# Attention with a routed layer: one load queue with three loads under way, casts of q and k on GpSimd, stores on ScalarE's queue, whole-block transposes

## The chip, the core and the metric

The kernel runs on one core of a Trainium2 chip. The metric is the device time of one execution in microseconds. A core has five engines with an instruction queue each: TensorE (PE in the profile), VectorE (DVE), ScalarE (ACT), GpSimd (POOL) and SyncE (SP). Each queue is worked off in order. DMAs are issued from a queue (here SP, ACT or POOL) and carried out by 16 DMA engines that all queues share.

## The reference

There are 4 batches, 8 heads, 768 positions and 64 values per head. A position sees the first 4 positions (the sinks) and the last 128. After attention the heads are put side by side to x (768 x 512 per batch), and the 128 positions of each batch with the highest score x . w_gate go through a small network.

```python
scores = scale * np.matmul(q, k.transpose(0, 1, 3, 2))
keep = is_sink | in_window          # pos < 4, or 0 <= rel < 128
a = softmax(np.where(keep, scores, -1e9))
x = np.matmul(a, v)                 # heads side by side: (B, 768, 512)
for b in range(B):
    top_idx = np.argpartition(-s[b], 128)[:128]      # s = x . w_gate
    ye = np.maximum(x[b, top_idx] @ w1, 0.0) @ w2    # 512 -> 1024 -> 512
    out[b, top_idx] = x[b, top_idx] + sigmoid(s[b, top_idx])[:, None] * ye
```

## The kernel before

A batch is cut into six blocks of 128 positions, and its heads into four pairs; two pairs make a group g. A `unit(b, j, gs)` handles block j of batch b for the groups gs. Batch 0 runs its six blocks for group 0 and then for group 1; the other batches run both groups at once. The order on every engine is the order in which the functions are called, since all engines are scheduled by hand.

In a unit, `close()` ends the block before it (the products with the sinks on TensorE, then reciprocal, x and the gate's junk reduction on VectorE: L385, L388, L399). `scores` multiplies k and q of the next block on TensorE (L290, L307) and takes the exponentials on ScalarE (L313). `pv_halves` and `pv` multiply the exponentials with v (L365, L378). `transposes` brings q and k of one pair of the next batch into shape: TensorE transposes 24 halves into PSUM (L254), VectorE copies KT (L258) and ScalarE QT (L260), and GpSimd copies the sinks' columns of KT (L262). `spread` sends the gate scores along a row (L412, and L413 on ScalarE). In batches 1 to 3 the steps of choosing and of the network for the batch before are put between: `moe_steps` gathers the 128 rows from the output in DRAM with an indirect DMA of GpSimd (L462), and `mlp_steps` adds its result to them with another (L494).

Data come in so. The q and k of batch 0's first two pairs are loaded as fp32 on SP (`load`, L93), and cast by ScalarE and VectorE (`casts`, L139, L140). All other q and k, 28 loads, are cast to bf16 on the way by DMAs that GpSimd issues (L125). v is loaded by SP, 30 loads, into two buffers with a pitch of 128 fp32 values per head. The 16 blocks of w1 and w2 are loaded by SP and cast by GpSimd a unit later (`cast_w`, L240). The function `loads` holds a plan that names for every unit which loads it issues, and ties each to the last exponential, or the last product with v, that was issued ahead of it. The stores of x stand on SP as well (`finish_block`, L395, and L397 for a second copy of batch 3).

```python
def load(out, in_, flight=3, gate=None):
    ins = nc.sync.dma_start(out=out, in_=in_)
    if gate is not None:
        wait_for(ins, gate)
    elif len(line) >= flight:
        wait_for(ins, line[-flight])
    line.append(ins)
```

So a load without a gate waits for the load three (or four) places before it. The framework gives every DMA issued from SP or ACT one of eight completion semaphores in turn, and makes a DMA wait until the last one that held its semaphore is done.

Of the kernel before, what the change touches and what calls it, by code (L numbers as in the profile page):

```python
# [17 lines left out]
B = 4  # L18
H = 8
# [12 lines left out]
def kernel(  # L32
# [16 lines left out]
    wp = ctx.enter_context(tc.tile_pool(name="wp", bufs=1))  # L49
    qkp = ctx.enter_context(tc.tile_pool(name="qkp", bufs=2))  # L50
    qbp = ctx.enter_context(tc.tile_pool(name="qbp", bufs=6))
    vp = ctx.enter_context(tc.tile_pool(name="vp", bufs=1))
# [10 lines left out]


    vbuf = [vp.tile([128, NB, H, 2 * D], FP32, name=f"vbuf{i}", tag=f"vbuf{i}") for i in range(2)]
    vsr = [vp.tile([128, D], FP32, name=f"vsr{i}", tag=f"vsr{i}") for i in range(2)]
# [24 lines left out]

    def load(out, in_, flight=3, gate=None):
        ins = nc.sync.dma_start(out=out, in_=in_)  # L93
        if gate is not None:
            wait_for(ins, gate)
        elif len(line) >= flight:
            wait_for(ins, line[-flight])
        line.append(ins)
# [13 lines left out]

    def load_qk(st, hp, t, gate=None):
        nm, src = (("k", k), ("q", q))[t]
        ob = qbp.tile([128, 2, NB, D], BF16, name=nm + "b", tag=nm + "b")
        st.kq[hp, t] = ob
        in_ = src[st.b, 2 * hp:2 * hp + 2, :, :].rearrange("h (p c) d -> p h (c d)", c=NB)
        flat = "p h c d -> p h (c d)"  # L120
        if st.b == 0 and hp < 2:
            f = st.kf[hp, t] = qkp.tile([128, 2, NB, D], FP32, name=nm + "f", tag=nm + "f")
            load(out=f[:, :, :, :].rearrange(flat), in_=in_, flight=4)
        else:
            ins = nc.gpsimd.dma_start(out=ob[:, :, :, :].rearrange(flat), in_=in_)  # L125
            if gate is not None:
                wait_for(ins, gate)

    def load_v(st, c, hs, flight=3, gate=None):
        load(out=st.v[:, c, hs, 0:D], in_=v[st.b, hs, c * 128:(c + 1) * 128, :].rearrange("h p d -> p h d"),  # L130
             flight=flight, gate=gate)

# [4 lines left out]

    def casts(st, hp):
        nc.scalar.copy(out=st.kq[hp, 0][:, :, :, :], in_=st.kf[hp, 0][:, :, :, :])  # L139
        nc.vector.tensor_copy(out=st.kq[hp, 1][:, :, :, :], in_=st.kf[hp, 1][:, :, :, :])  # L140

# [8 lines left out]
    for hp in (0, 1):  # L150
        for t in range(2):
            load_qk(st0, hp, t)

# [41 lines left out]
    for c in (1, 2):  # L195
        load_v(st0, c, slice(0, 4))


# [33 lines left out]

    def load_w(i, gate):
        src = moe_w1[128 * (i // 2):, 512 * (i % 2):] if i < 8 else moe_w2[128 * (i - 8):, :]
        wf[i] = qkp.tile([128, 512], FP32, name="wf", tag="kf" if i % 2 else "qf")
        load(out=wf[i][:, :], in_=src[0:128, 0:512], gate=gate)

    def cast_w(i):
        dst = w1_sb[:, i // 2, 512 * (i % 2):512 * (i % 2) + 512] if i < 8 else w2_sb[:, i - 8, :]
        nc.gpsimd.affine_select(out=dst, in_=wf[i][:, :], compare_op=ALU.is_ge, fill=0.0,  # L240
                                base=0, pattern=[[0, 512]], channel_multiplier=0)

# [3 lines left out]
    def transposes(st, hp):  # L246
# [3 lines left out]
        for t, (src, dst) in enumerate(((st.kq[hp, 0], st.KT), (st.kq[hp, 1], st.QT))):  # L250
            trp = ps.tile([128, 8, 128], BF16, name="trp", tag="ps")
            for c in range(NB):
                for h in range(2):
                    nc.tensor.transpose(out=trp[es[h], c, :], in_=src[:, h, c, :], identity=ident_b[:])  # L254
            o = dst[:, hp, :].rearrange("d (p c) -> d p c", c=NB)
            i = trp[:, 0:NB, :].rearrange("d c p -> d p c")
            if t == 0:
                nc.vector.tensor_copy(out=o, in_=i)  # L258
            else:
                nc.scalar.copy(out=o, in_=i)  # L260
# [99 lines left out]
    def pv_halves(st, j, gs):  # L360
        for g in gs:
            for hh in range(4):
                for m in range(2):
                    f = first(st, j, g, m)
                    ins = nc.tensor.matmul(out=st.xg[j, g][es[m], hh, :],  # L365
                                           lhsT=prob(st, j - m, g, hh, es[m], 3 * m),
                                           rhs=st.v[es[m], j - m, 4 * g + hh, 0:VS], **f)
                    fence(st, j, gs, ins, 8 * gs.index(g) + 2 * hh + m, 8 * len(gs))
# [3 lines left out]
    def pv(st, j, g):  # L372
        terms = {0: [(0, 0), (0, 1)], 1: [(0, 2), (0, 3), (1, 0), (1, 1)]}.get(j, [(j - 1, 2), (j, 1)])
        for hh in range(4):
            for i, (kc, s) in enumerate(terms):
                m = i % 2
                f = first(st, j, g, m)
                late[0] = nc.tensor.matmul(  # L378
                    out=st.xg[j, g][es[m], hh, :], lhsT=prob(st, kc, g, hh, slice(0, 128), s),
                    rhs=st.v[:, kc, 4 * g + hh, 0:VS], **f)  # L380

    def normalize(st, j, g):
# [8 lines left out]
        if g == 1:  # L391
            finish_block(st, j)

    def finish_block(st, j):
        nc.sync.dma_start(out=out[st.b, j * 128:(j + 1) * 128, :], in_=st.x[j][:, :])  # L395
        if st.b == B - 1:
            nc.sync.dma_start(out=x_last[j * 128:(j + 1) * 128, :], in_=st.x[j][:, :])  # L397
        junk = mp.tile([128, DM], BF16, name="junk", tag="junk")
# [202 lines left out]


    qk_loads = {0: ([2], []), 1: ([3], [4]), 2: ([5], [6]), 3: ([7], [])}
    qk_loads_2 = {4: ([0], []), 5: ([1], [])}
    qk_loads_0 = {(i // 6, i % 6): ([i - 2], []) for i in range(2, 10)}

    w_loads = {(1, 3): 1, (1, 4): 1, (1, 5): 1, (2, 0): 1, (2, 2): 1, (2, 3): 1, (2, 4): 3, (2, 5): 3, (3, 0): 4}
    w_next = iter(range(16))
    w_casts = []

    def loads(b, j, gs, end):
        gate = late[0] if end else exps[-1]
        plans = [(b + 1, qk_loads.get(j) if b else qk_loads_0.get((gs[0], j)))]
        if 1 in gs:
            plans.append((b + 2, qk_loads_2.get(j)))
        for s, plan in plans:
            for i in plan[end] if plan and s < B else ():
                load_qk(states[s], i // 2, i % 2, gate)
        if end:
            for i in w_casts:  # L620
                cast_w(i)
            w_casts.clear()
            for _ in range(w_loads.get((b, j), 0)):
                i = next(w_next)
                load_w(i, gate)
                w_casts.append(i)
        nxt = states.get(b + 1)
        if end:
            return
        if b == 0:  # L630

            if gs == (0,) and j < 3:
                load_v(st0, j + 3, slice(0, 4), gate=gate)
            c = j - 2 if gs == (0,) else j + 4
            if 0 <= c < NB:
                load_v(st0, c, slice(4, 8), gate=gate)
        if nxt and 1 in gs:
            load_v(nxt, j, slice(0, H), gate=gate)
            if j == 0:
                load_sinks(nxt)  # L640

# [13 lines left out]
    def unit(b, j, gs):  # L655
        st = states[b]
        last = 1 in gs
        end = (b, j) == (B - 1, NB - 1)
        ahead = states.get(b + 1) if last else None
        close()  # L660
        if j == 0:
            for g in gs:
                scores(st, 1, g)
                pv(st, 0, g)
                normalize(st, 0, g)
            loads(b, j, gs, 0)
            pack_sinks(st, gs)
            sink_scores(st, gs)
        elif end:
# [7 lines left out]
            for g in gs:  # L677
                normalize(st, j, g)
            cast_x(st, j)
        else:  # L680
# [3 lines left out]
            elif ahead:  # L684
                scores(ahead, 0, 0)
            loads(b, j, gs, 0)
            if j >= 2:
# [24 lines left out]
        if b == B - 1 and j and not end:  # L712
            cast_x(st, j - 1)
        if last:
            loads(b, j, gs, 1)
        if ahead and j == 5:
# [6 lines left out]
    keep_warm(10)  # L723
    for hp in range(2):
        casts(st0, hp)
        transposes(st0, hp)
        for t in range(2):
            load_qk(st0, 2 + hp, t)
        keep_warm(3)
    scores(st0, 0, 0)  # L730
    wg_ps = ps.tile([128, DM], FP32, name="wg_ps", tag="ps")
    nc.tensor.matmul(out=wg_ps[:, :], lhsT=one[:, :], rhs=wg[:, :], start=True, stop=True)
    nc.vector.tensor_copy(out=wgb[:, :], in_=wg_ps[:, :])
    constants()
    for g in range(2):
        for j in range(NB):
            unit(0, j, (g,))
        if g == 0:
            scores(st0, 0, 1)
    for b in range(1, B):  # L740
        select[b - 1] = moe_steps(states[b - 1])
        mlp[b - 1] = mlp_steps(states[b - 1])
        for j in range(NB):
            unit(b, j, (0, 1))
# [36 lines left out]
```

## Time and profile before

| what | value |
|---|---|
| median of 3 runs (lowest to highest) | 148.12 us (146.75 to 152.5) |
| profiled execution: time, span | 147.8 us, 146.1 us |
| TensorE busy in matmuls | 126.4 us, 87% of the span |
| VectorE, ScalarE, GpSimd busy | 90.3, 78.8, 52.6 us |
| granted TensorE clock, mean | 0.971 |
| DMA queues: hardware, software | 19.96 MB at 47.4%, 7.21 MB at 34.7% of 16 engines' span |
| instruction transfers of 16 KB | 23 |
| matmuls and weight loads | 2,923 each |
| chain that ended last | PE 64%, issue 11%, ACT 9%, DMA 6% |

A row of a time line gives the start in us, the length in us, the engine, the line of the kernel, the operation, the tiles it writes and reads, and in brackets how long the engine was idle before and what ended that. "issue" there means that the profile shows nothing the engine waited for. A row of the list of groups gives the number of instructions, their busy time, the mean of one in ns, and the idle time before them. In the rows of windows come the length, the busy time and the number of instructions of PE, its weight loads, DVE, ACT and POOL, then the granted clock, the busy share of the DMA engines and GB/s. The rows of 40 slices give tenths, 3.65 us a slice.

### The profile page before, as it was taken

Reading aid. Unit: us, or ns where it says so; the run is one execution under the profiler, and the core shown is the slowest. Engines: PE = TensorE matmul, PEld = TensorE weight load, DVE = VectorE, ACT = ScalarE, POOL = GpSimd, SP = SyncE. Lnnn points to the kernel's source line nnn. Section 1 sums busy time; section 2 is a strip of 40 time slices with the busy share of each in tenths; the row PEclk is TensorE's granted clock in tenths of the full one; section 3 lists DMA queues with packets and bytes.
Section 4 is the critical chain, followed back from the end, with each engine's and each line's share of the span. In section 5 each row is a group of like instructions: output and inputs, shape, how many; then the busy total and the mean of one; then the engine's idle time right before and its main releaser. Section 6 shows DMA issues by size and latency. Waiting matters only on the chain.

```text
span 146.1 us, 6782 instructions
## 1 busy us (share of the span) xinstructions
PE 126.4 (87%) x2923; PEld 99.1 (68%) x2923; DVE 90.3 (62%) x294; ACT 78.8 (54%) x168; POOL 52.6 (36%) x111
## 2 busy tenths in 40 slices
PE   6859997996979999888999967799999999999900
PEld 2335886685867897777779846597896886586600
DVE  5635444565977987767699836376994624794120
ACT  3448552963658666653875823348763872542300
POOL 5467143142330525232251380405525240424320
PEclk9999999999999999999999999779999999999985
DMA  4969499399999899999759999966796456391701
GB/s 143 295 106 210 102 149 187 69 191 238 280 266 230 189 196 273 200 288 272 179 75 268 263 223 227 304 227 193 216 252 254 115 101 194 79 244 48 125 19 72
DMA packets 41600, 27.61 MB, mean 189 GB/s; under 512 B 26593, under 2 KB 35169, under 8 KB 41570
## 3 DMA queue, kind: packets, MB, share of 16 engines
q1 hardware_dynamic: 32930, 19.96, 47.4%
q0 software_dynamic: 8640, 7.21, 34.7%
q8 instruction: 23, 0.38, 1.0%
q14 instruction: 7, 0.06, 0.1%
HBM read 24.15 MB, written 8.91 MB: 226 GB/s over the span
## 4 chain that ended last, share of the span: by engine, by line
PE 64%; issue 11%; ACT 9%; DMA 6%; DVE 3%; POOLq 1%; SPq 1%; POOL 1%; ACTq 0%
PE xg L378 17%; PE xg L365 11%; PE trp L254 8%; ACT pt L313 7%; PE sc L290 7%; PE xg L350 6%; DMA qf<-in_q_dram 4%; PE sc L307 3%; PE bc L412 3%; PE hps L482 3%; PE ye L488 2%; DMA out_dram<-gye,idx 2%; DVE cm L418 1%; ACT psk L324 1%; SPq L93 1%
## 5 line engine op out<-in xcount | busy, mean ns | idle before, releaser
L313 ACT ACTIVATE pt<-sc 128x448 f32<-128x448 f32 (+2 forms) x96 | 44.4, 551 | 10.3 <-PE sc L307 9.9
L378 PE MATMUL xg<-vbuf,pt 128*64 128x65 f32 x896 | 34.4, 226 | 0.2 <-ACT pt L313 0.2
L378 PEld LDWEIGHTS xg<-vbuf,pt 128*64 128x64 f32 x896 | 29.4, 137 | 4.4 <-issue 1.6
L260 ACT COPY QT<-trp 128x768 bf16<-128x768 bf16 x16 | 12.8, 798 | 27.4 <-PE trp L254 27.4
L365 PE MATMUL xg<-vbuf,pt 64*64 64x65 f32 x512 | 22.1, 226 | 2.4 <-issue 2.0
L258 DVE COPY KT<-trp 128x768 bf16<-128x768 bf16 x16 | 15.3, 956 | 12.5 <-PE trp L254 12.5
L365 PEld LDWEIGHTS xg<-vbuf,pt 64*64 64x64 f32 x512 | 20.0, 140 | 3.2 <-issue 2.2
L290 PE MATMUL sc<-QT,KT 64*64 64x192 bf16 (+3 forms) x384 | 20.8, 255 | 0.8 <-issue 0.4
L388 DVE TENSOR_TENSOR x<-xg,rz 128x256 f32<-128x256 f32 x48 | 20.4, 424 | 1.7
L385 DVE RECIPROCAL rz<-xg 128x4 f32<-128x4 f32 x48 | 8.5, 176 | 19.3 <-PE xg L350 17.5
L307 PE MATMUL sc<-msk,ident_b 64*64 64x256 bf16 (+1 forms) x256 | 17.7, 258 | 0.2 <-issue 0.2
L399 DVE CUSTOM_DVE_ANT_0 junk<-x,wgb 128x512 bf16<-128x512 f32 x24 | 16.9, 706 | 0.8
L290 PEld LDWEIGHTS <-KT 64*64 64x64 bf16 x384 | 11.7, 107 | 8.0 <-issue 4.0
L125 POOL DMA_DIRECT2D kb<-in_k_dram x14 | 10.3, 734 | 16.1 <-ACT pt L313 16.1
L418 DVE SCALAR_TENSOR_TENSOR cm<-sbc,scol,tie 128x128 bf16<-128x128 f32 (+5 forms) x23 | 15.3, 664 | 0.1
L262 POOL TENSOR_SCALAR_AFFINE_SELECT ksk<-KT 64x4 bf16<-64x4 bf16 x32 | 6.0, 188 | 25.5 <-DVE KT L258 19.0
L240 POOL TENSOR_SCALAR_AFFINE_SELECT w_sb<-wf 128x512 bf16<-128x512 f32 x16 | 10.5, 662 | 12.9 <-DMA wf<-in_moe_w_dram 12.5
L254 PE MATMUL trp<-ident_b,kb 128*64 128x128 bf16 x192 | 9.1, 221 | 6.6 <-issue 5.3
L125 POOL DMA_DIRECT2D qb<-in_q_dram x14 | 10.1, 718 | 11.2 <-ACT pt L313 11.2
L350 PE MATMUL xg<-vsk,psk 64*64 64x260 f32 x128 | 13.9, 416 | 0.0
L254 PEld LDWEIGHTS <-kb 128*64 128x64 bf16 x192 | 6.4, 110 | 8.3 <-issue 5.9
L307 PEld LDWEIGHTS <-ident_b 64*64 64x64 bf16 x256 | 10.0, 109 | 0.5 <-issue 0.5
(113 smaller groups left out, 148.8 us busy)
## 6 DMA issues: line engine op xcount, KB each, us to landing
out_dram<-x SPq DMA_DIRECT2D x24, 256.0 KB, 4.2
vbuf<-in_v_dram SPq DMA_DIRECT2D x18, 256.0 KB, 4.5
wf<-in_moe_w_dram SPq DMA_DIRECT2D x16, 256.0 KB, 6.4
kb<-in_k_dram POOLq DMA_DIRECT2D x14, 192.0 KB, 5.8
qb<-in_q_dram POOLq DMA_DIRECT2D x14, 192.0 KB, 5.9
vbuf<-in_v_dram SPq DMA_DIRECT2D x12, 128.0 KB, 4.4
x_last<-x SPq DMA_DIRECT2D x6, 256.0 KB, 3.3
kf<-in_k_dram SPq DMA_DIRECT2D x2, 384.0 KB, 4.5
```

Of the source, the lines that this page charges most:

```text
L125: ins = nc.gpsimd.dma_start(out=ob[:, :, :, :].rearrange(flat), in_=in_)
L254: nc.tensor.transpose(out=trp[es[h], c, :], in_=src[:, h, c, :], identity=ident_b[:])
L258: nc.vector.tensor_copy(out=o, in_=i)
L290: nc.tensor.matmul(out=sc[e][es[kh], hh * w + q0:hh * w + q1], lhsT=st.KT[es[e], hp, k0 + 64 * kh:k0 + 64 * kh + 64], rhs=st.QT[es[e], hp, ...
L307: nc.tensor.matmul(out=sc[e][es[kh], o:o + 2 * w].rearrange("p (h s n) -> p h s n", h=2, n=64)[:, :, sq, :], lhsT=ident_b[es[e], es[e]], r ...
L313: exps.append(nc.scalar.activation(out=pt[:, e, 0:n], in_=sc[e][:, 0:n], func=ACT.Exp, scale=0.125))
L350: ins = nc.tensor.matmul(out=st.xg[j, g][es[m], :, :], lhsT=st.psk[es[g], q0:q0 + 64], rhs=st.vsk[es[g], :, :], **f)
L365: ins = nc.tensor.matmul(out=st.xg[j, g][es[m], hh, :], lhsT=prob(st, j - m, g, hh, es[m], 3 * m), rhs=st.v[es[m], j - m, 4 * g + hh, 0:VS ...
L378: late[0] = nc.tensor.matmul(out=st.xg[j, g][es[m], hh, :], lhsT=prob(st, kc, g, hh, slice(0, 128), s), rhs=st.v[:, kc, 4 * g + hh, 0:VS], ...
L388: nc.vector.tensor_tensor(out=st.x[j][:, 256 * g:256 * g + 256].rearrange("p (h d) -> p h d", h=4), in0=xg[:, :, 0:D], in1=rz[:, :, :].to_ ...
L399: nc.vector.tensor_tensor_reduce(out=junk[:, :], in0=st.x[j][:, :], in1=wgb[:, :], scale=1.0, scalar=0.0, op0=ALU.mult, op1=ALU.add, accum ...
L418: nc.vector.scalar_tensor_tensor(out=cm[:, :], in0=st.sbc[:, 0:n], scalar=st.scol[:, j:j + 1], in1=tie[:, S - n:S], op0=ALU.subtract, op1= ...
```

## The change

The loads of q and k are all plain fp32 loads on SP now. The whole of batch b + 1 is put on SP's queue at the start of batch b (`load_batch`): eight loads of q and k, then six of v, with the 16 blocks of the weights between v of batch 3. A load waits only for the load three places before it (four in two places of batch 0), and for its buffer. The casts of q and k, but those of the first two pairs, go to GpSimd (`cast`), two instructions a tensor, one unit ahead of the transposes. q and k are kept with the two heads of a pair side by side, so that TensorE transposes a whole block of 128 x 128 at once, 12 for a pair. v lies with a pitch of 65 values. The stores of batches 0 to 2 are issued from ScalarE's queue (`stores`), right after the exponentials of a unit; those of batch 3 stay on SP. Half of the casts of the weights go to ScalarE, and all 16 are made at three places. At the start, three warming matmuls are gone and the gate weights' matmul stands ahead of the first scores.

```diff
-    qkp = ...(name="qkp", bufs=2)   qbp = ...(name="qbp", bufs=6)
+    qkp = ...(name="qkp", bufs=6)   qbp = ...(name="qbp", bufs=3)
-    vbuf = [vp.tile([128, NB, H, 2 * D], FP32, ...) for i in range(2)]
+    vbuf = [vp.tile([128, NB, H, VS], FP32, ...) for i in range(2)]
...
-    def load_qk(st, hp, t, gate=None):
...
-        if st.b == 0 and hp < 2:
-            f = st.kf[hp, t] = qkp.tile([128, 2, NB, D], FP32, ...)
-            load(out=f..., in_=in_, flight=4)
-        else:
-            ins = nc.gpsimd.dma_start(out=ob..., in_=in_)
+    def load_qk(st, hp, t, flight=3):
+        nm, src = (("kf", k), ("qf", q))[t]
+        f = st.kf[hp, t] = qkp.tile([128, 2, NB, D], FP32, name=nm, tag=nm)
+        load(out=f..., in_=src[...], flight=flight)
...
+    def cast(st, hp, t):
+        nm = ("kb", "qb")[t]
+        o = st.kq[hp, t] = qbp.tile([128, NB, 2, D], BF16, name=nm, tag=nm)
+        o, i = o[:, :, :, :].rearrange("p c h d -> p h c d"), st.kf[hp, t]
+        if st.b == 0 and hp < 2:
+            (nc.vector.tensor_copy if t else nc.scalar.copy)(out=o, in_=i[:, :, :, :])
+            return
+        for e in range(2):
+            nc.gpsimd.affine_select(out=o[:, e, :, :], in_=i[:, e, :, :], compare_op=ALU.is_ge, fill=0.0,
+                                    base=0, pattern=[[0, NB], [0, D]], channel_multiplier=0)
+    def load_batch(st):
+        for hp in range(HP):
+            for t in range(2):
+                load_qk(st, hp, t)
+        w = iter(range(16)) if st.b == B - 1 else iter(())
+        for c in range(NB):
+            load_v(st, c, slice(0, H))
+            if c == 0:
+                load_sinks(st)
+            for i in (next(w, None) for _ in range(4)):
+                if i is not None:
+                    load_w(i)
...
+    for i in range(4):                       # batch 0, after v 0 to 2 of group 0
+        load_qk(st0, 2 + i // 2, i % 2)
+        if i < 3:
+            load_v(st0, 3 + i, slice(0, 4))
+    for c in range(NB):
+        load_v(st0, c, slice(4, 8), 4)
...
     def cast_w(i):
+        if i % 2:
             nc.gpsimd.affine_select(out=dst, in_=wf[i][:, :], ...)
+        else:
+            nc.scalar.copy(out=dst, in_=wf[i][:, :])
...
-                for h in range(2):
-                    nc.tensor.transpose(out=trp[es[h], c, :], in_=src[:, h, c, :], identity=ident_b[:])
+                nc.tensor.transpose(out=trp[:, c, :], in_=src[:, c, :, :].rearrange("p h d -> p (h d)"),
+                                    identity=ident_b[:])
...
+    def stores():
+        for st, j in done:
+            rows = slice(j * 128, (j + 1) * 128)
+            if st.b < B - 1:
+                nc.scalar.dma_start(out=out[st.b, rows, :], in_=st.x[j][:, :])
+            else:
+                nc.sync.dma_start(out=out[st.b, rows, :], in_=st.x[j][:, :])
+                nc.sync.dma_start(out=x_last[rows, :], in_=st.x[j][:, :])
+        done.clear()
     def finish_block(st, j):
-        nc.sync.dma_start(out=out[st.b, j * 128:(j + 1) * 128, :], in_=st.x[j][:, :])
+        done.append((st, j))
...
-    qk_loads, qk_loads_2, qk_loads_0, w_loads and def loads(b, j, gs, end)
+    w_casts = {(2, 5): range(0, 4), (3, 0): range(4, 9), (3, 1): range(9, 16)}
...
     def unit(b, j, gs):
+        if ahead and 1 <= j <= 4:
+            for t in range(2):
+                cast(ahead, j - 1, t)
         close()
         if j == 0:
             for g in gs:
                 scores(st, 1, g)
+                stores()
                 pv(st, 0, g)
                 normalize(st, 0, g)
-            loads(b, j, gs, 0)
...
                 scores(ahead, 0, 0)
-            loads(b, j, gs, 0)
+            stores()
...
-        if last:
-            loads(b, j, gs, 1)
+        for i in w_casts.get((b, j), ()):
+            cast_w(i)
...
-    for hp in range(2):
-        casts(st0, hp)
-        transposes(st0, hp)
-        ...
-        keep_warm(3)
-    scores(st0, 0, 0)
-    wg_ps = ...
+    cast(st0, 0, 0)
+    cast(st0, 0, 1)
+    cast(st0, 1, 0)
+    transposes(st0, 0)
+    keep_warm(3)
+    cast(st0, 1, 1)
+    transposes(st0, 1)
+    wg_ps = ...
+    scores(st0, 0, 0)
...
     for g in range(2):
+        if g:
+            load_batch(states[1])
         for j in range(NB):
+            if g == 0 and j in (2, 3):
+                for t in range(2):
+                    cast(st0, j, t)
             unit(0, j, (g,))
...
     for b in range(1, B):
+        if b + 1 < B:
+            load_batch(states[b + 1])
```

## The prediction

> **What bounds the kernel now.** I read the busy shares over 40 slices first, then the list of DMA issues, then windows of single stretches, then the time lines of TensorE, ScalarE and SyncE. The profiled execution took 147.8 us: a span of 146.1 and 1.7 around it. It stands 0.3 under the median of 148.12; I sum against 147.8 and add the 0.3 at the end.
>
> ```profile
> PE   6859997996979999888999967799999999999900
> PEclk9999999999999999999999999779999999999985
> DMA  4969499399999899999759999966796456391701
> ```
>
> TensorE has no long holes from slice 4 to slice 36, and the DMA engines are as full as it is until about slice 29 (106 us), when the loads end. So two things are near their limit at once.
>
> ```profile
> 3.90:5.30 1.40, 1.40 (x13) 0.49 (x13) 0.67 (x4) 0.83 (x1) 0.57 (x4) 1.00 0.85 275
> 5.30:7.60 2.30, 1.60 (x27) 0.73 (x21) 1.45 (x2) 0.80 (x1) 1.37 (x5) 1.00 0.89 284
> 44.00:70.00 26.00, 24.30 (x689) 20.73 (x683) 19.82 (x63) 16.35 (x37) 8.89 (x19) 1.00 1.12 234
> ```
>
> The last column is GB/s. In the two early windows almost only plain q and k loads are under way: they move about 280. In the third, which is batch 1, the mix moves 234 at a DMA share over 1.
>
> ```profile
> out_dram<-x SPq DMA_DIRECT2D x24, 256.0 KB, 4.2
> vbuf<-in_v_dram SPq DMA_DIRECT2D x18, 256.0 KB, 4.5
> wf<-in_moe_w_dram SPq DMA_DIRECT2D x16, 256.0 KB, 6.4
> kb<-in_k_dram POOLq DMA_DIRECT2D x14, 192.0 KB, 5.8
> vbuf<-in_v_dram SPq DMA_DIRECT2D x12, 128.0 KB, 4.4
> kf<-in_k_dram SPq DMA_DIRECT2D x2, 384.0 KB, 4.5
> ```
>
> The last number is the median from issue to landing: 4.4 to 4.5 us for plain loads of any size.
>
> ```profile
> 35.55 0.49 PE L254 MATMUL trp<-ident_b,kb 128*64 128x128 bf16 x11 [1.23 <-issue]
> 85.92 0.47 PE L254 MATMUL trp<-ident_b,kb 128*64 128x128 bf16 x9 [1.39 <-issue]
> 92.30 0.30 PE L254 MATMUL trp<-ident_b,kb 128*64 128x128 bf16 x3 [1.84 <-issue]
> ```
>
> These pauses begin in the middle of a run of transposes, so no operand is missing. Counting weight loads and matmuls together, the pauses fall on instruction 193 or 194 after a multiple of 256, and each follows one of the 23 instruction transfers of 16 KB in the trace: TensorE has run out of instructions. There are seven, 0.80 + 1.23 + 1.03 + 0.43 + 0.99 + 1.39 + 1.84 = 7.7 us, 4.5 of it before 70 us. After the last, the granted clock falls to 0.50 (94 to 96 us), 0.81 and 0.89 beside it: (1 - 0.81) x 2 + (1 - 0.50) x 2 + (1 - 0.89) x 3 = 1.7 us more.
>
> **The change, part by part.** The part that decides is a wait. In both built programs every DMA on the two hardware queues signals one of eight completion semaphores, dealt out in turn, and a DMA that takes one again first waits for its last holder. Before, loads and stores all stood on SyncE, so that wait held up SyncE alone. Now the 18 stores of batches 0 to 2 stand on ScalarE, and the holder is mostly a load. Numbering SyncE's loads 1 to 78 without the sinks and the gate weights (1-20 batch 0; 21-28 q and k, 29-34 v of batch 1; 35-42 and 43-48 batch 2; 49-56 q and k of batch 3; then v and w mixed), the built program makes ScalarE wait as follows. "Due" is where the store falls in the trace of before: the start of the last exponential ahead of it.
>
> | store (batch, block) | due, us | waits for load |
> |---|---|---|
> | (0,1) | 30.8 | 26, q of pair 2, batch 1 |
> | (0,2) | 33.7 | 29, v, batch 1 |
> | (0,5) | 45.7 | 35, k of pair 0, batch 2 |
> | (1,1) | 52.7 | 42, last q of batch 2 |
> | (1,4) | 65.8 | 54, q of pair 2, batch 3 |
> | (1,5) | 71.6 | 58, first w |
> | (2,0) | 75.0 | 61, fourth w |
>
> Behind a waiting store stand the copy to QT, the copy of the score row and the next exponentials; TensorE waits for these. When do the loads land? Load 4 lands at 8.7 (VectorE's cast starts there). Loads 5 to 20: by bandwidth 4 x 393 KB at 280 GB/s (1.40 us) and 12 half v at 0.62 (below) give 13.0, so 21.7; by landing, ten at 4.4 / 3 and six at 4.4 / 4 (four under way) give 21.3, so 30.0. I take 26, the middle: those landings were measured beside casting loads, which are gone. Loads 21 to 58 are 38: by landing 4.5 / 3 = 1.50 us each, 57. By bandwidth: 24 q and k at 1.40 = 33.6; 13 v of 1024 pieces of 256 bytes, 19 ns a piece on 16 engines in the trace = 1.24, so 16.1; one w 0.75; 11 stores between them, 128 pieces at 94 ns = 0.75 each, 8.3; together 58.8. The two agree, so load 58 lands at 26 + 57 = 83. It is due at 71.6: **+11.4**. Load 61, three w later at 1.1, lands at 86.3, due 75.0: +11.3. Loads 26, 35, 42 and 54 land at 35, 48.5, 59 and 77, that is 4, 3, 6 and 11 late: the loss builds up in batch 1. After load 61 the stores wait on loads that are several units old, and no more is lost.
>
> Bounds: if stores cost the loads nothing and the start goes by bandwidth, load 58 lands at 21.7 + 50.5 = 72.2 (+0.6); with casting-load landings of 5.8, at 30 + 38 x 1.93 = 103 (+32). I take 1.50, since v and kf are the same instructions.
>
> The v pieces now lie 260 bytes apart instead of 512, so they no longer start on round addresses. No row shows such a piece. Ends: nothing; or twice 19 ns, 1.24 more for each of 13 loads and 0.62 for 12 halves, +23.6 on load 58. I take nothing, as the piece is as long as before, and let the range reach part of the way. The Trainium skill (DMA: Bandwidth & Descriptors, "How a descriptor splits into AXI transactions") speaks against this pitch: a transfer that starts off a 256-byte boundary fetches bytes it does not use. By its beats I estimate 15 cycles in place of 11 for each piece, +8.5 us on load 58, and a sum of about 166; no run so far shows it.
>
> ScalarE gains 18 issues and eight casts of w.
>
> ```profile
> 28.12 0.37 SPq L395 DMA_DIRECT2D out_dram<-x  x1
> 99.60 3.04 ACT L313 ACTIVATE pt<-sc 128x512 f32<-128x512 f32 x6 [0.31 <-PE sc L307]
> L407 ACT CAST xb<-x 128x512 bf16<-128x512 f32 x6 | 3.7, 620 | 1.7 <-DVE x L388 1.7
> L240 POOL TENSOR_SCALAR_AFFINE_SELECT w_sb<-wf 128x512 bf16<-128x512 f32 x16 | 10.5, 662 | 12.9 <-DMA wf<-in_moe_w_dram 12.5
> ```
>
> An issue takes SyncE 0.37, so 18 x 0.37 = 6.7; a cast of this size takes ScalarE 0.62, eight 5.0. ScalarE goes from 78.8 to 90.5 busy. Nearly all lies where ScalarE idles for transposes (27.4 us before QT); the store issues fall in waits already counted. Two casts stand right before the six exponentials of the turn from batch 2 to 3 (99.60), which run without a gap: 1.2. The other six come in threes, 1.9, beside units of some 5 us: 0.3. **+1.5**; ends 0 and 11.7.
>
> GpSimd loses 28 issues (20.4 us by their rows) and eight w casts (5.3), and gains 56 casts of 128x384: 662 x 384 / 512 = 0.50 each, 27.8. It stays near 36% busy; a unit's four casts take 2.0 of some 5 us, one unit ahead of their transposes. Nothing; if that cover goes, up to 2.0 a unit. A cast that waits for its load also holds the sink copies and the gather of the chosen rows behind it, a unit before they are needed. VectorE can be held by a cast: one junk reduction beside a w cast took 983 ns instead of 691; 24 x 0.3 is off the path at 62% busy.
>
> A pair's transposes go from 24 halves in 0.67 us (two at a time) to 12 whole ones, at 59 ns as the 32 hps matmuls in 1.89: 0.71. Sixteen times +0.04 is nothing. But TensorE's stream loses 384 of 5,846 instructions, in its densest place, and the casting queue is gone. Of the pauses left after 70 us (3.2) and the clock loss (1.7) I take **-3.0**; ends 0 and -4.9. The earlier pauses lie inside waits for loads. The Trainium skill (Runtime: NRT & Kernel Launch, "Instruction fetch mechanics") calls the crossing of a 16 KiB block mostly hidden; here seven crossings cost 7.7 us, so the trace decides. By the page nothing would be won and the sum would be 161.
>
> At the start, three warming matmuls go (0.75 us) and the gate-weight matmul moves ahead of the first scores; the load chain does not start sooner, so 0. SyncE loses the 18 stores; batch 3's stand behind load 78, which lands a few units before it is used.
>
> Sum: 147.8 + 11.4 + 1.5 - 3.0 = 157.7, plus 0.3: **158**.
>
> **Rivals.** *Loads keep ahead (faster).* If load 58 lands by 71.6 - 4.5 = 67.1, ScalarE never waits and the pauses go: 147.8 - 7.7 - 1.7 - 0.75 + 1.5 = 139.2. It needs (67.1 - 26) / 38 = 1.08 us a load. For: casting loads are gone and less is duplicated in flight. Against: 1.40 us for q and k at the best rate seen.
>
> *Loads just in time (no change).* At about 1.2 us a load, load 58 lands at 71.6 and nothing is lost or won before 70: 147.8 + 1.5 - 3.0 = 146.3.
>
> *Slow v pieces (much slower).* The pitch doubles them: 158 + 23.6 = 182; a third of that, 166. For: no row excludes it. Against: the pieces keep their number and length.
>
> *GpSimd's casts come late.* The q of pair 3 (load 14) lands near 22; two casts make it 23; its transposes were due at 22.5. A wait of 1 us, inside the +11.4.
>
> **How the numbers follow.** Stores behind loads at 1.3 to 1.75 us each (150 to 167): 0.64. Slow v or slower loads still: 0.13. Just in time: 0.14. Keeping ahead: 0.09. A measurement of this kernel tells about 2% from no change, 145.2 to 151.1; a small part of the first case falls in it. So faster 0.08, same 0.15, slower 0.77. The range leaves out the rival at 139 and the slow end of v: 148 to 169; the likeliest case alone has 150 to 167.
>
> **What would show it.** Right: ScalarE's longest waits end at DMA landings of kf, qf, vbuf or wf ahead of the store line, 5 us and more in batch 1's last two blocks; the turn to batch 2 some 11 us later than 71.6; afterwards units as long as before, with fewer pauses in the transposes. SyncE's loads 21 to 58 spaced 1.5 us. Wrong: ScalarE's store issues without waits, or loads spaced near 1.1 us; v packets well over 19 ns would move the loss to v; a TensorE waiting for GpSimd's casts would be another mechanism.

## The result and the profile after

The changed kernel takes 158.72 us at the median (157.38 to 159.5, 4 runs); beside it on the same chip the kernel before took 147.44 (146.43 to 152.5, 4 runs). The ratio is 1.078, with a 95% interval of 1.066 to 1.090. The profiled execution took 158.69 us, with a span of 156.9 and a granted clock of 0.949 (before: 147.8, 146.1 and 0.971). Here and below a ratio with an interval compares undisturbed executions only, so it need not be the quotient of the medians of all executions beside it; where too few were undisturbed no ratio is given.

The busy shares over 40 slices of 3.92 us, the kernel after:

```profile
PE   6679989873979859999509899999999999999920
PEclk9999999999699995999965999999999999999997
DMA  4868756998999989998979799569579355284521
```

TensorE now has holes: at 35 to 39 us, 55 to 59 and, widest, 75 to 82 (the digits 3, 5 and 50). The granted clock falls to 0.50 in or behind each of them: from 38.6 to 42.0 us, 59.1 to 62.5 and 79.6 to 86.4. The DMA engines are as full as before meanwhile. From 82 us on TensorE is full again. The chain that ended last by engine, and from the list of waits (us in total, times, longest) the ones that matter:

```profile
DMA 50%; PE 29%; issue 5%; ACT 4%; DVE 4%; POOL 3%; SPq 2%; POOLq 1%; ACTq 1%
```

```profile
ACT QT L278 <- DMA qf<-in_q_dram: 11.4, 2, 6.3
POOL kb L135 <- DMA kf<-in_k_dram: 11.3, 5, 4.7
...
PE sc L308 <- ACT QT L278: 7.2, 2, 6.0
```

DMA went from 6% of the chain to 50%; GpSimd's casts wait for k, ScalarE's QT for q, TensorE for QT. A copy to QT reads PSUM that TensorE filled; no load of q can be its operand. Its wait "for qf" is that of the store issued just ahead of it. ScalarE's time line shows this:

```profile
74.34 1.12 ACT L331 ACTIVATE pt<-sc 128x512 f32<-128x512 f32 x2
81.27 0.40 ACTq L420 DMA_DIRECT2D out_dram<-x  x1
81.71 0.80 ACT L278 COPY QT<-trp 128x768 bf16<-128x768 bf16 x1 [6.26 <-DMA qf<-in_q_dram]
82.41 0.27 ACT L443 COPY sbc<-bc 128x128 f32<-128x128 f32 x1
83.41 1.08 ACT L331 ACTIVATE pt<-sc 128x512 f32<-128x512 f32 x2 [0.73 <-PE sc L325]
84.91 1.08 ACT L331 ACTIVATE pt<-sc 128x512 f32<-128x512 f32 x2 [0.42 <-PE sc L325]
87.42 0.35 ACTq L420 DMA_DIRECT2D out_dram<-x  x1
```

The store of block (1,4) stands behind the exponentials that end at 75.46, and is issued at 81.27, when load 54 (a q) lands. SyncE's load 57, which waits for load 54 by the rule of three under way, goes in the same moment:

```profile
81.27 0.37 SPq L92 DMA_DIRECT2D vbuf<-in_v_dram  x1
```

QT follows the store, and TensorE's next scores follow QT:

```profile
76.27 0.30 PE L308 MATMUL sc<-QT,KT 64*64 64x256 bf16 x4
82.56 0.42 PE L308 MATMUL sc<-QT,KT 64*64 64x256 bf16 x4 [5.99 <-ACT QT L278]
```

The next store, of (1,5), waits again, for load 58. SyncE issues that load at 83.15, and the store goes at 87.42:

```profile
83.15 4.54 SPq L92 DMA_DIRECT2D wf<-in_moe_w_dram  x4
```

The loads do not keep up although all is plain now. Windows of the stretches between loads 21, 35, 49 and 58 (the columns are those of the windows before):

```profile
24.66:46.02 21.36, 17.00 (x332) 13.61 (x323) 12.68 (x38) 10.22 (x22) 10.23 (x22) 0.92 0.93 267
46.02:68.04 22.02, 18.22 (x423) 15.15 (x423) 14.31 (x44) 11.90 (x27) 9.35 (x17) 0.92 0.91 257
68.04:83.15 15.11, 9.11 (x230) 7.92 (x226) 6.89 (x21) 5.10 (x13) 7.52 (x19) 0.88 0.89 270
```

More bytes move than the 234 GB/s of batch 1 before, yet the DMA share is 0.89 to 0.93 where it was over 1. The issues and their median time to landing, which is a median over the few whose landing the trace names (two of k, four of q):

```profile
kf<-in_k_dram SPq DMA_DIRECT2D x16, 384.0 KB, 3.7
qf<-in_q_dram SPq DMA_DIRECT2D x16, 384.0 KB, 4.8
out_dram<-x ACTq DMA_DIRECT2D x18, 256.0 KB, 4.5
vbuf<-in_v_dram SPq DMA_DIRECT2D x18, 256.0 KB, 4.2
wf<-in_moe_w_dram SPq DMA_DIRECT2D x16, 256.0 KB, 3.6
```

To see where the 10.8 us of span came from I set the same exponentials of both traces beside each other (after less before):

| start in before, us | 28.5 | 33.3 | 47.8 | 56.4 | 65.4 | 70.2 | 74.5 | 83.0 | 95.3 | 103.1 | 114.6 | 120.5 |
|---|---|---|---|---|---|---|---|---|---|---|---|---|
| delay, us | -0.9 | +4.5 | +4.7 | +7.9 | +9.0 | +13.2 | +15.8 | +15.4 | +11.1 | +12.9 | +11.1 | +11.1 |

The loss grows to 15.8 at the turn to batch 2; 4.7 come back by 95 us.

### The profile page after: what moved, and what is told of

The parts are those of the page before. It is cut to its first block, busy times and chain, and to the rows that moved or that the text cites. A ratio compares the mean times of both kernels' runs of the same rounds, so it can differ in the third digit from the quotient of the medians.

```text
span 156.9 us, 6463 instructions
## 1 busy us (share of the span) xinstructions
PE 129.8 (83%) x2724; PEld 102.1 (65%) x2728; DVE 92.2 (59%) x294; ACT 82.0 (52%) x176; POOL 60.3 (38%) x131
## 3 DMA queue, kind: packets, MB, share of 16 engines
q0 software_dynamic: 1024, 1.70, 6.8%
## 4 chain that ended last, share of the span: by engine, by line
DMA 50%; PE 29%; issue 5%; ACT 4%; DVE 4%; POOL 3%; SPq 2%; POOLq 1%; ACTq 1%
DMA qf<-in_q_dram 18%; DMA vbuf<-in_v_dram 15%; PE xg L396 8%; DMA kf<-in_k_dram 8%; PE xg L383 5%; DMA xe<-out_dram,idx 4%; PE xg L368 3%; PE sc L308 2%; DMA x_last<-x 2%; PE hps L512 2%; PE ye L518 2%; PE trp L271 2%; ACT pt L331 2%; DMA out_dram<-gye,idx 2%; DVE x L406 1%
## 5 line engine op out<-in xcount | busy, mean ns | idle before, releaser
L396 PE MATMUL xg<-vbuf,pt 128*64 128x65 f32 x896 | 36.4, 232 | 0.7 <-ACT pt L331 0.7
L396 PEld LDWEIGHTS xg<-vbuf,pt 128*64 128x64 f32 x896 | 31.0, 143 | 5.8 <-issue 1.9
L308 PE MATMUL sc<-QT,KT 64*64 64x192 bf16 (+3 forms) x384 | 22.5, 259 | 10.7 <-ACT QT L278 7.2
L308 PEld LDWEIGHTS <-KT 64*64 64x64 bf16 x384 | 12.7, 108 | 18.6 <-issue 14.2
L448 DVE SCALAR_TENSOR_TENSOR cm<-sbc,scol,tie 128x128 bf16<-128x128 f32 (+5 forms) x23 | 16.7, 727 | 6.6 <-ACT sbc L443 6.5
L135 POOL TENSOR_SCALAR_AFFINE_SELECT kb<-kf 128x384 bf16<-128x384 f32 x28 | 15.8, 587 | 11.7 <-DMA kf<-in_k_dram 11.3
L135 POOL TENSOR_SCALAR_AFFINE_SELECT qb<-qf 128x384 bf16<-128x384 f32 x28 | 16.1, 599 | 7.1 <-DMA qf<-in_q_dram 4.3
L271 PE MATMUL trp<-ident_b,qb 128*128 128x128 bf16 x96 | 8.2, 223 | 5.2 <-ACT QT L278 3.5
L443 ACT COPY sbc<-bc 128x128 f32<-128x128 f32 x23 | 6.3, 275 | 9.2 <-PE bc L442 3.8
L271 PEld LDWEIGHTS <-qb 128*128 128x128 bf16 x96 | 6.2, 100 | 6.0 <-issue 3.6
```

Of the source, the lines that this page charges most:

```text
L135: nc.gpsimd.affine_select(out=o[:, e, :, :], in_=i[:, e, :, :], compare_op=ALU.is_ge, fill=0.0, base=0, pattern=[[0, NB], [0, D]], channel ...
L271: nc.tensor.transpose(out=trp[:, c, :], in_=src[:, c, :, :].rearrange("p h d -> p (h d)"), identity=ident_b[:])
L308: nc.tensor.matmul(out=sc[e][es[kh], hh * w + q0:hh * w + q1], lhsT=st.KT[es[e], hp, k0 + 64 * kh:k0 + 64 * kh + 64], rhs=st.QT[es[e], hp, ...
L396: late[0] = nc.tensor.matmul(out=st.xg[j, g][es[m], hh, :], lhsT=prob(st, kc, g, hh, slice(0, 128), s), rhs=st.v[:, kc, 4 * g + hh, :], **f)
L448: nc.vector.scalar_tensor_tensor(out=cm[:, :], in0=st.sbc[:, 0:n], scalar=st.scol[:, j:j + 1], in1=tie[:, S - n:S], op0=ALU.subtract, op1= ...
```

## The experiments

The lost time could come from ScalarE's stores waiting for loads, from ScalarE's extra work, or from the pace of the loads whatever the stores do. The gain was put down to fewer pauses of TensorE for instructions. "The pauses" below are the waits of TensorE's stream once in 256 instructions. With matmuls, weight loads and the stream's few semaphore instructions counted together, all seven pauses of the kernel before fall on place 193 of 256.

**The stores alone, in the kernel before.** The 18 stores go to ScalarE at the places of the change; loads, casting DMAs and plan stay.

```diff
+    done = []
+    def stores():                    # as in the change, at the same places
...
-        nc.sync.dma_start(out=out[st.b, j * 128:(j + 1) * 128, :], in_=st.x[j][:, :])
+        done.append((st, j))
```

> The kernel before with one part of the change alone: the 18 stores stand on ScalarE's queue, at the same places as in the changed kernel; loads keep their gates. In the built program a store's semaphore was held by a load that was issued a unit or more earlier, by a sink load or by another store. Theory A: hardly any waits for loads, within 2 us of before (146 to 150), in spite of 18 issues on ScalarE. Theory C: 18 x 0.37 = 6.7 us on ScalarE, 152 to 155. Theory B: no change from before.

149.24 us (145.75 to 149.67, 4 runs), beside 149.81 (146.22 to 153.0, 13 runs) for before: no difference that these runs can tell. Each issue took ScalarE about 0.34 us, as here:

```profile
68.45 0.34 ACTq L400 DMA_DIRECT2D out_dram<-x  x1
71.61 0.80 ACT L260 COPY QT<-trp 128x768 bf16<-128x768 bf16 x1 [2.87 <-PE trp L254]
```

QT's wait ends at TensorE's transposes, not at a DMA. So issuing from ScalarE costs nothing that shows by itself; the loss needs late loads in the same ring of semaphores.

**The stores on GpSimd, in the changed kernel.** Stores there take no semaphore of that ring.

```diff
-                nc.scalar.dma_start(out=out[st.b, rows, :], in_=st.x[j][:, :])
+                nc.gpsimd.dma_start(out=out[st.b, rows, :], in_=st.x[j][:, :])
```

> The changed kernel with the 18 stores of batches 0 to 2 issued from GpSimd's queue in place of ScalarE's; the loads, casts and transposes stay. In the built program these stores wait for x and, three times over, for an older store, never for a load. Theory A (ScalarE waits for loads that held a store's semaphore): the waits are gone, time 139 to 146 us, ScalarE's QT copies follow their transposes, SyncE's loads keep their spacing of about 1.6 us. Theory B (the loads of q, k and v themselves come too late for the casts and products, wherever the stores stand): 155 to 160 us, TensorE and GpSimd wait for loads instead. Theory C (the cost is the issuing of DMAs and the casts on ScalarE): between, some 152 us, as 6.7 of the 10 us come off.

151.72 us (149.09 to 155.35, 10 runs), ratio 1.020 (1.012 to 1.028). The delay against before never passes 2.0 us up to 88 us and is -2.2 at 100: the 15.8 are gone, as the theory of the store's wait says. But 8.5 us are lost at the turn to batch 3 (-2.2 at 101.5, +2.3 at 103.1, +6.3 at 108.8). ScalarE's time line there:

```profile
100.89 1.22 ACT L259 CAST w_sb<-wf 128x512 bf16<-128x512 f32 x2
104.88 0.62 ACT L259 CAST w_sb<-wf 128x512 bf16<-128x512 f32 x1 [2.77 <-DMA wf<-in_moe_w_dram]
105.40 1.84 ACT L331 ACTIVATE pt<-sc 128x448 f32<-128x448 f32 x4
```

Now the weights are late: casts of w that wait for their loads stand ahead of the exponentials. Load 76 was issued at 110.57. The loads were spaced 1.69 us, slower still than the 1.58 of the change; why is open. The profiled execution took 153.33 us, 1.6 over the median, so part of the 8.5 may be its own. The expectation was half right: the waits and the 15.8 are gone, the 139 to 146 us did not come. The time is the 152 that was put down to issues and casts on ScalarE, but the issues cost nothing in the run before, and the 7.3 us that ScalarE lost ahead of its casts of w were waits for loads.

**More loads under way.** `flight=3` becomes 4 or 6; stores stay on ScalarE.

```diff
-    def load(out, in_, flight=3):
+    def load(out, in_, flight=6):
```

> The changed kernel with four loads under way. Latency form of A: the spacing of loads 21 to 58 was 1.58 us with three and 1.38 with six; with four between, some 1.45, which brings the first w in 5 us sooner: 151 to 155 us. Bandwidth form: spacing as with three, 156 to 159.

> The changed kernel with six loads under way instead of three (the six v loads of batch 0 that had four keep four). Theory A in its bandwidth form (loads 21 to 58 run at what the DMA engines give, 257 to 270 GB/s in the trace): the first w lands at most 3 us sooner, 156 to 159 us. Theory A in its latency form (three loads per 4.5 us): spacing falls below 1.3 us, the loads come ahead of ScalarE, 143 to 150 us. Theory B gives the same two ends. Theory C: no change.

| loads under way | spacing of loads 21 to 58, us | load 58 issued | largest delay | median, us |
|---|---|---|---|---|
| 3 (the change) | 1.58 | 83.15 | +15.8 | 158.72 |
| 4 | 1.49 | 76.9 | +10.3 | 152.37 (149.66 to 153.95, 5 runs), ratio 1.021 (1.003 to 1.038) |
| 6 | 1.375 | 70.23 | +4.5 | 147.02 (146.94 to 149.15, 4 runs), ratio 0.986 (0.957 to 1.014) |

With six, one constant takes back what the change lost, as far as the interval tells. Load 58 is 12.9 us earlier; 5.3 of that are won before load 21 (issued at 19.36 instead of 24.66), the rest by the spacing. The single load then takes longer, but more of them overlap: the five among loads 21 to 58 whose landing the trace names took 4.8 to 9.2 us, and five with three under way 3.8 to 5.8. In the list of issues the medians rest on one k and two q:

```profile
kf<-in_k_dram SPq DMA_DIRECT2D x16, 384.0 KB, 5.7
qf<-in_q_dram SPq DMA_DIRECT2D x16, 384.0 KB, 6.5
```

The store's wait is still there (ScalarE's time line, six under way), once instead of twice:

```profile
71.35 0.34 ACTq L420 DMA_DIRECT2D out_dram<-x  x1
71.73 0.80 ACT L278 COPY QT<-trp 128x768 bf16<-128x768 bf16 x1 [5.89 <-DMA qf<-in_q_dram]
```

From load 21 to load 58 the DMA engines moved 264 GB/s with three under way and 310 with six. So three under way is what set the pace of 1.58; the bandwidth was not used up.

**The casts of w off ScalarE**, stores on ScalarE as in the change (first run), and together with stores on GpSimd (second run).

```diff
-        if i % 2:
-            nc.gpsimd.affine_select(out=dst, in_=wf[i][:, :], ...)
-        else:
-            nc.scalar.copy(out=dst, in_=wf[i][:, :])
+        nc.gpsimd.affine_select(out=dst, in_=wf[i][:, :], ...)
```

> The changed kernel with all 16 casts of the weights on GpSimd. Theory A: the only gain is at the turn from batch 2 to 3, where two casts stand ahead of the exponentials: 1.6 us in the traces, so 157 to 158 us. Theory C: eight casts at 0.62 on ScalarE, 5 us, so 153 to 154.

161.13 us (158.49 to 161.49), ratio to before 1.071 (1.025 to 1.117): no better than the change. The exponentials of the turn came 1.4 us sooner against their neighbours, and the end did not.

> The changed kernel with three loads under way, the 18 stores and all casts of w on GpSimd. In the run with the stores alone on GpSimd, ScalarE lost 7.3 us in waits for w loads ahead of its casts. Theory A: the exponentials no longer stand behind those waits, so part of it comes back, 144 to 148 us; what is left is the network waiting for w itself. Theory B (the loads are too late for their use, whoever casts): 149 to 153 us as with the stores alone, TensorE waiting at hps and ye.

151.11 us (150.32 to 152.31), ratio 1.030 (1.016 to 1.045). It was 4.1 us ahead of before at 99.6 and 2.6 behind at 120: SyncE issued the loads of w as late as 109.35, and GpSimd waited for them 7.6 us in sum. With three under way the weights come too late whoever casts them.

**Where the pauses went.** The changed kernel has none over 0.3 us (1.2 us in sum; before has 10.9 by the same count, which takes every step of the whole stream at such a place). Six under way had 3.4. These sums run about from start to start, so some 1 us stands even where TensorE never stops; its idle time alone at these places is 7.9 us before, 0.05 in the change and 1.6 with six. Two runs: six under way with the stores on GpSimd, and six under way (stores on ScalarE) with 24 half transposes a pair again.

```diff
-                nc.tensor.transpose(out=trp[:, c, :], in_=src[:, c, :, :].rearrange("p h d -> p (h d)"),
-                                    identity=ident_b[:])
+                for h in range(2):
+                    nc.tensor.transpose(out=trp[es[h], c, :], in_=src[:, c, h, :], identity=ident_b[:])
```

> The changed kernel with six loads under way and the 18 stores on GpSimd's queue. If the loads' pace (A) is the root, and ScalarE's stores and its casts of w are the two places where it is felt, both are relieved: 139 to 145 us, below before. If six under way had taken off all there was (147 in the run with six alone), the stores' move adds nothing: 146 to 149. If the DMA bandwidth binds (loads 21 to 58 no closer than 1.38 us, w late again): 147 to 150, with ScalarE's casts of w waiting for DMAs.

149.98 us (149.28 to 151.22), ratio 1.020 (1.004 to 1.035): a miss, by 5 us for the first theory. The time lies in the range for a binding bandwidth, whose sign, casts on ScalarE that wait for DMAs, did not show. The waits for loads were gone, but the pauses were back, nine over 0.3 us and 12.5 us in sum (9.1 of idle time), without casting loads and with whole transposes. Three of them on TensorE's time line:

```profile
67.61 0.92 PE L383 MATMUL xg<-vbuf,pt 64*64 64x65 f32 x24 [1.86 <-issue]
73.77 0.35 PE L308 MATMUL sc<-QT,KT 64*64 64x192 bf16 x6 [0.90 <-issue]
79.57 0.45 PE L463 MATMUL cs<-minus,cm 128*128 128x1 bf16 x12 [0.73 <-issue]
```

They now fall into products with v and scores, not only into transposes.

> The changed kernel with six loads under way, and with the 24 half transposes of a pair put back in place of 12 whole ones: 384 more instructions on TensorE, the loads stay plain. Theory P (the pauses for instructions came from the density of TensorE's stream): pauses over 0.3 us return, 7 to 11 us in all as in before, 150 to 154 us. Theory Q (they came from the casting loads, whose pieces held the instruction transfers back): pauses stay at some 2 to 4 us, and 146 to 149 us as with six loads alone.

150.69 us (150.25 to 151.53), ratio 1.026 (1.012 to 1.039), where the same kernel with whole transposes had 0.986. The pauses rose from 3.4 to 6.5 us (1.6 to 4.3 of idle time). So the density of the stream counts, and it is not the whole cause. The traces show one step more. Wherever before or the run with six and stores on GpSimd has a pause over 0.5 us, the instruction transfer started 3.0 to 4.8 us after TensorE had passed the last such place; it took 0.9 to 1.2 us, as without a pause, and TensorE went on 1.2 to 1.7 us after its end. In the change they started within 3.1 us of such a place. What fits all runs: a pause comes when the instruction transfer has to queue among many loads and TensorE meanwhile runs at full speed through its 256 instructions. In the change itself TensorE is held up by late loads, and has time to fetch. The late start is measured; that the loads cause it is drawn from the order of the runs, and no run moved the instruction transfer alone.

**Four and five under way, stores and all casts of w on GpSimd.** The two edits to GpSimd above, and:

```diff
-    def load(out, in_, flight=3):
+    def load(out, in_, flight=4):
```

> The change with four loads under way instead of three, and both the stores of batches 0 to 2 and all casts of w on GpSimd. With three under way this form took 151.1 us: ahead of the kernel before by up to 4 us until 100 us, then 6 lost as the weights' loads ended late. With four the loads are 0.09 us closer (1.49 instead of 1.58), so the 40 or so loads between load 21 and the weights should land some 4 us sooner. Theory A (the loads' spacing is what is left at the turn to batch 3): 145 to 148, and the exponentials of the last turn no more than 1 us behind the kernel before. Rival (the instruction pauses of TensorE come back as the queues fill, 12.5 us of them with six under way and stores on GpSimd): 149 to 152, with pauses over 5 us in sum.

148.85 us (147.32 to 150.74, 10 runs), ratio 1.001 (0.995 to 1.006), between the two ranges. The rival's pauses came (4.0 us of idle time), but the lead was lost elsewhere: the profiled execution was 4.0 us ahead at 104 and 3.5 behind at 108.8. VectorE's time line in that place, then GpSimd's:

```profile
97.01 0.99 DVE L426 CUSTOM_DVE_ANT_0 junk<-x,wgb 128x512 bf16<-128x512 f32 x1
97.94 0.08 DVE L426 DVE_READ_ACCUMULATOR2_ANT scol<- 128x1 f32 x1
97.94 7.60 DVE L445 SCALAR_TENSOR_TENSOR cm<-sbc,scol,tie 128x640 bf16<-128x640 f32 x1
```

```profile
97.42 0.56 POOL L417 DMA_DIRECT2D out_dram<-x  x1
97.98 6.87 POOL L255 TENSOR_SCALAR_AFFINE_SELECT w_sb<-wf 128x512 bf16<-128x512 f32 x12
```

In the same run a comparison with 768 columns took 1.01 us while GpSimd was idle; this one, of 640, which took 0.88 in the kernel before, took 7.60 and ended 0.69 us after the last of twelve casts in a row. TensorE then waited 5.5 us for VectorE:

```profile
106.16 2.00 PE L393 MATMUL xg<-vbuf,pt 128*64 128x65 f32 x32 [5.52 <-DVE x L403]
```

> As the run with four loads under way, both stores and w casts on GpSimd, but five under way. Theory A alone: 143 to 146, since spacing falls to about 1.43. The rival (pauses come back): 148 to 151, with sum of pauses between that of four and the 12.5 us of six.

152.39 us (148.74 to 153.71, 4 runs), with the same comparison at 7.61 us and pauses of 7.1 us. Both theories missed this hold.

**Four and five under way, stores on GpSimd, casts of w half and half as in the change.** The last form without the edit of the casts.

> The change with four loads under way and the stores of batches 0 to 2 on GpSimd; the casts of w stay half on ScalarE and half on GpSimd. With all 16 casts on GpSimd this form was 4 us ahead of the kernel before at 103 us and then lost 7.5: one comparison of VectorE took 7.6 us instead of about 1, for as long as 12 casts of w ran on GpSimd without a gap. Theory: with half of the casts on ScalarE, GpSimd never runs so many in one piece, the comparison stays near 1 to 2 us, and what is left of the lead is 4 less 1.5 for ScalarE's casts: 143.5 to 146.5. Rival (the loss at that place is late w loads or pauses, whoever casts): 148 to 151.

144.99 us (142.28 to 147.0, 6 runs), beside 149.48 (144.71 to 152.54, 11 runs) for before: 3.0% less by the medians, 1.7% less by the fastest of each, no ratio given. The profiled execution took 142.28, with a span of 140.6. Its busy shares:

```profile
PE   6978999969989999969998999999979999899900
PEclk9999999999999999999999999999999999999996
DMA  4979967999699999998999999999792554390711
```

TensorE has no hole as wide as those of the change, and the clock was 0.992. Pauses were 2.75 us in sum. The comparison, with GpSimd's casts behind it:

```profile
94.89 3.22 DVE L448 SCALAR_TENSOR_TENSOR cm<-sbc,scol,tie 128x640 bf16<-128x640 f32 x1
```

```profile
95.11 2.31 POOL L256 TENSOR_SCALAR_AFFINE_SELECT w_sb<-wf 128x512 bf16<-128x512 f32 x4
```

Again it ended 0.69 us after the last cast, four of them this time: 3.22, where I had expected 1 to 2. This is the lowest median of all the runs; that it beats the kernel before is likely, but not settled by executions whose ranges overlap.

> As the run with four under way and the stores on GpSimd, but five under way. If pace alone counted: 142 to 146. With the pauses of TensorE that five and six under way showed (6 to 12 us in sum): 146 to 149. The comparison of VectorE beside w's casts again 1 to 2 us.

147.32 us (145.46 to 150.18, 6 runs). The loads are closer (1.36 us against 1.52 with four), but pauses take 8.1 us (5.2 of idle time, against 0.7 with four). The comparison took longer again, with five casts in a row beside it (VectorE, then GpSimd):

```profile
99.28 3.78 DVE L448 SCALAR_TENSOR_TENSOR cm<-sbc,scol,tie 128x640 bf16<-128x640 f32 x1
```

```profile
99.50 2.88 POOL L256 TENSOR_SCALAR_AFFINE_SELECT w_sb<-wf 128x512 bf16<-128x512 f32 x5
```

Four is the better compromise between late loads and pauses.

With the stores on SyncE, at the same places behind the plain loads, the program's waits block each other (a deadlock), so this placement has no time and stays open.

## Why the prediction was right, and where its terms were off

**The deciding wait: right in mechanism, too small.** Stores of ScalarE waiting for the load that held their semaphore are what the time lines show, with the loads named: in all seven cases below the store goes within 0.07 us of SyncE's load three places further on, which waits for the same landing. With the stores on GpSimd the delay never passed 2.0 us up to 88 us. The steps of the chain:

| store waits for load | 26 | 29 | 35 | 42 | 54 | 58 | 61 |
|---|---|---|---|---|---|---|---|
| predicted landing, us | 35 | 39.5 | 48.5 | 59 | 77 | 83 | 86.3 |
| store issued, us | 36.5 | 40.5 | 50.4 | 62.5 | 81.3 | 87.4 | 91.0 |

The term was +11.4; measured +15.8. Of the 4.4 missing, 1.5 stand at load 26 already; the rest is the spacing from there on, (87.4 - 36.5) / 32 = 1.59 instead of 1.50. The landing of 4.5 was about right, but it was a median of a few: "plain loads of any size" passed over the 6.4 us of w, in the same rows. The five among loads 21 to 58 whose landing the trace names took 4.7 us at the mean, a third of which is 1.57; where SyncE is seen to wait for a landing, the next issue follows 0.01 to 0.02 us after it. So few landings do not settle how much of the rest is the landing and how much the order of SyncE's issues. The 26 us for load 20, the middle between two estimates that lay 8 us apart, came close by luck: load 23, which waits for it, was issued at 26.63. That "the two agree", bandwidth and landing, was chance too: with six under way the same loads came every 1.375 us, so bandwidth did not bind at 1.5. The half clock behind each hole had no term in the sum; it falls where the work waits for loads anyway.

**The rivals with loads ahead or just in time** needed 1.08 and 1.2 us a load. Six under way gave 1.375, so three could give neither. *GpSimd's casts come late* happened about as priced (1 us): load 14 landed at 21.61, and TensorE waited 0.68 us for its cast, until 22.81, ahead of the larger waits.

**The v pieces: nothing, as taken.** In the packets of the two traces a 256-byte piece takes 18.6 ns at the new pitch and 18.9 at the old. The estimate of +8.5 from the Trainium skill (DMA: Bandwidth & Descriptors, "How a descriptor splits into AXI transactions") is not borne out for pieces that lie unaligned in SBUF. They changed only on the side where they are written, and the page's sentence is on bytes fetched. (1024 pieces of 19 ns on 16 engines are 1.22 us, not 1.24; it changes nothing.)

**The casts of w on ScalarE: +1.5, measured 0.** ScalarE's exponentials came 1.56 us later at the turn (from +11.32 to +12.88), as the term says. But TensorE did not: at its next selection matmuls (L452 before, L482 after) it stood 122.06 - 110.91 = +11.15, and ScalarE was back at +11.1 by 114.6. The step failed at "run without a gap": no gap in ScalarE's work does not put it on the path. Moving these casts to GpSimd alone won nothing.

**The pauses: -3.0, measured -4.7**, near the -4.9 of the far end. The 4.7 is all that the stretch from 75 to 95 us regained; the kernel before has two pauses there (1.39 and 1.84) and the half clock from 93.2 to 96.6, and the change has neither. The place 193 is the same for all seven pauses only if semaphore instructions are counted too; by weight loads and matmuls alone it drifts from 184 to 160. The size was off, and so was half of the reason: "the casting queue is gone" does not end them, for they return without it when enough plain loads are queued (12.5 us). The other half, the denser stream, is borne out by the run with half transposes.

**GpSimd's casts** take 587 to 599 ns instead of 500, and GpSimd is busy 60.3 us; in the change no wait of TensorE shows that they held up anything beyond the late loads. "VectorE can be held by a cast" was priced at 0.3 us each and held there; in the form with twelve casts in a row it was 6.7 us and on the path. The Trainium skill (SBUF — State Buffer, "Who interferes with whom") says that a VectorE instruction with two inputs in SBUF and a GpSimd instruction that reads SBUF exclude each other. The 7.60, 3.78, 3.22 and (three under way, stores and casts on GpSimd) 3.05 us agree, with twelve, five, four and four casts, and show that the wait is for the whole run of casts, not for one.

By the measured terms: 147.8 + 15.8 - 4.7 - 0.3 (the end) + 0.1 (around the span) = 158.7. The total of 158 was close in part by luck, since errors offset each other: the load term was 4.4 short, against 1.5 for casts that never came and 1.7 more regained.

## What to carry to other kernels

Before a DMA is moved to a compute engine's queue, list what each issue will wait for beyond its data: here a completion semaphore held by an unrelated load stopped exponentials for up to 6 us, while the same stores in a kernel whose loads were early cost nothing. A limit on loads under way is a pace: with three it was about a third of a landing, 1.58 us a load, and that has to stay under the time in which the work uses a load up. Tune the two together, since each wait that is removed exposes the next one (late stores, late weights, VectorE held by GpSimd, instruction pauses), and judge each on the path of TensorE, not on the engine that does the work.

## What was not expected of the hardware

- The single queue's spacing went 1.58, 1.49, 1.375 us a load with three, four and six under way, with landings of 3.8 to 5.8 us at three and 4.8 to 9.2 at six, five named by each trace.
- TensorE's pauses for instructions rose from 1.2 us (three under way, stores on ScalarE) to 12.5 (six under way, stores on GpSimd) with nearly the same instructions; of idle time alone from 0.05 to 9.1.
- A VectorE comparison was held 6.7 us by twelve GpSimd casts in a row, and ended 0.69 us after the last of them, at four casts as at twelve (0.68 at five).
